# A different hand-out of the work made ahead in a gated layer: value sets, transposes, and weight decoding

## The chip, the cores and the metric

The kernel runs on one core of a Trainium2 chip. The metric is the time of one execution in microseconds (us), as the device measures it. The core's engines work side by side, each through its own queue and in program order: TensorE (PE in the profile, with PEld for its weight loads), VectorE (DVE), ScalarE (ACT), GpSimd (POOL), and SyncE (SP), which here issues most DMAs. They wait for one another through semaphores.

## The reference

The kernel computes three stages one after the other, on 4 x 576 = 2304 tokens of width 512.

```python
scores = scale * q @ k.T;  scores = where(causal, -1e9, scores + decay)      # 4 batches, 8 heads, 576 x 64
x      = softmax(scores) @ v                                                 # -> 2304 x 512
e      = argmax(x @ w_gate + modality_bias[modality_id])                     # one of 8 experts for a token
x      = prob[e] * (relu(x @ w1[e]) @ w2[e])                                 # 512 -> 1024 -> 512
gate   = 1 / (1 + exp(-(x @ moe2_w_gate)))                                   # 512 -> 1536
val    = x @ moe2_w_val                                                      # 512 -> 1536
out    = (gate * val) @ moe2_w_out                                           # 1536 -> 512
```

The three matrices of the last stage are float64 in the input and reach the kernel as pairs of 32-bit words.

## The kernel before

All large products are made in a split form: a float32 matrix is taken apart into a high part (rounded by ScalarE) and a low part (the remainder, by VectorE), and high x high, high x low and low x high are added up in PSUM. So each weight or activation that TensorE reads costs one ScalarE and one VectorE operation first.

**Decoding.** The float64 weights of the gated layer are 36 pieces of 128 x 512 values. `Gated.decode` (L1149) takes a piece through load (SP), one ScalarE operation (L1174), two VectorE operations in its first half (L1155, L1156) and two in its second (L1165, L1166), and a write back to DRAM as float32 (L1161). It is called in halves, and it works as a pipeline: the second half of a call also loads a later piece. The first `AHEAD` pieces are decoded while the experts run: the function `extra` (L1552) is called after each of the eight steps f of an expert unit and gives out as many halves as the table `pace` says for that step. The rest is given out in the gated layer.

**The gated layer** (`Gated.run`, L1429) goes over three strips s of 768 tokens. In a strip there are 12 sets: for each of six column pieces i a gate set (m = 0) and a value set (m = 1). Sets are numbered g = 0 to 35 over all strips, and q = 0 to 11 within a strip. Even sets are gate sets. Sets 0 to 3 make eight products of 6 matmuls directly (`eight`). From set 4 on, `seven` forms the four outputs of a set from seven products of 6 matmuls, called P0 to P6 here, on sums and differences of blocks. The products use two PSUM banks in turn, and what was in a bank must have been read out before the next product goes into it:

- P0 is copied out by ScalarE (L1358) before P2 is added onto it. P2 and P3 are copied out too.
- after P1, P4 and P5, VectorE adds a copied product to the one in PSUM (L1367, L1377, L1380). The add after P4 must have read the bank before P6 is added onto it. The add after P5 must have read its bank before the first product of the next set.
- the last output is read straight out of the bank, by ScalarE's sigmoid (L1337) in a gate set and by VectorE's multiplication with the gate (L1344) in a value set. A value set also splits its four results (L1345, L1346).

**Between the products** the generator yields, and the loop in `run` gives out other work in small portions: `bulk`, a queue of VectorE and ScalarE work made ahead (the next set's weights from `prepare`: L1202, L1205 and the four sums L1214 to L1223; the output weights: L1241, L1244; decode halves; block sums and splits of the next strip: L1292, L1304, L1308), and `outs`, the output products or downs (L1409, 3 matmuls each, 12 after each value set). A portion of `bulk` is its length divided by the steps left in the set (`left`).

**Transposes.** The next strip's 768 rows are loaded (`rows`, L1253), and transposed by `turn` (L1275): three TensorE transposes into one of the two product banks (L1279), a ScalarE copy out of it (L1284). There are eight turns for a strip. In what follows T is a turn and d a down.

Within an engine the order of the program is the order of execution, so work of `bulk` that stands ahead of an add delays this add, and the product that waits for its bank.

Of the kernel before, what the change touches and what calls it, by code (L numbers as in the profile page):

```python
# [29 lines left out]
KD = DM // P  # L30
# [1073 lines left out]
class Gated:  # L1104
# [8 lines left out]
    NB, NH = 768, 384  # L1113
    NP, NS = FF2 // 256, NT // 768

    DIRECT, AHEAD = 4, 24

    STEPS = (0, 0), (1, 1), (4, 2), (3, 3), (5, 4), (6, 5), (2, 6)

# [307 lines left out]
    def run(self, ctx):  # L1427
        self.lp = ctx.enter_context(self.tc.tile_pool(name="ga_l", bufs=1, reuse_waits="tile"))
        self.pp = ctx.enter_context(self.tc.tile_pool(name="ga_p", bufs=1, space=PSUM, reuse_waits="tile"))  # L1429
        self.po = ctx.enter_context(self.tc.tile_pool(name="ga_o", bufs=1, space=PSUM, reuse_waits="tile"))  # L1430
        self.todo.extend(self.late)
        self.flip, self.sg, self.act, self.acts, self.o = 0, {}, {}, {}, {}
        self.defer, outs, bulk = deque(), deque(), deque()
        nset, spare, rests = 2 * self.NP, deque([0, 1] * (len(self.late) + 4)), []
        self.outer_load(0)
        for g, (s, i, m) in enumerate(self.sets):
            q, p = g % nset, self.NP * s + i
            more = s + 1 < self.NS
            if 1 < g + 2 < len(self.sets):
                self.fetch(g + 2)  # L1440
            if m == 1 and p + 1 < self.NP * self.NS:
                self.outer_load(p + 1)
            bulk.extend(self.prepare(g + 1) if g + 1 < len(self.sets) else [])
            if m == 0:
                bulk.extend(self.outer(p))
            if s == 0:
                for _ in range(min(3 if m else 5, len(spare))):
                    bulk.append(lambda h=spare.popleft(): self.decode((h,)))
            if g == 0:
                bulk.extend(self.sums(0))  # L1450
            if g == 2:
                bulk.extend(self.split(0, 2) + self.split(0, 1)[2:] + self.split(0, 3) + self.split(0, 4))
            if more and q == 1:
                self.rows(s + 1)
            if more and q == 4:
                bulk.append(lambda s=s: self.tokens(s + 1))
            if more and q == 8:
                bulk.extend(self.sums(s + 1) + self.split(s + 1, 0))
            if more and q == 10:
                bulk.extend(self.split(s + 1, 1) + self.split(s + 1, 2) + self.split(s + 1, 3))  # L1460
            left = 8 if g < self.DIRECT else 7
            for k, w in enumerate((self.eight if g < self.DIRECT else self.seven)(g)):
                for f in rests:
                    f()
                rests = list(self.defer)
                self.defer.clear()

                x = []
                if g == self.DIRECT - 1 and k == 2:
                    x = self.split(0, 6)  # L1470
                if more and q == nset - 1 and k == 4:
                    x = self.split(s + 1, 4)
                if s and q == 0 and k < 2:
                    x = self.split(s, 5 + k)
                for f in x:
                    f()
                for _ in range(-(-len(bulk) * w // left)):
                    bulk.popleft()()
                left -= w
                for _ in range(w):  # L1480
                    if outs and (len(outs) > 7 - k or not (m == 0 and k in (2, 5) and w == 1)):
                        outs.popleft()()
            if m == 1:
                self.acts[p], self.act = self.act, {}
                order = ((0, 0), (1, 1), (0, 1), (1, 0)) if i + 1 < self.NP else ((1, 1), (0, 1), (0, 0), (1, 0))
                todo = [(r, n, j) for r, n in order for j in range(3)]
                if g + 1 == len(self.sets):
                    todo = [(r, n, j) for n in (1, 0) for j in range(3) for r in ((1, 0) if n else (0, 1))]
                outs.extend(lambda s=s, p=p, z=z: self.down(s, p, *z) for z in todo)
            if more and 3 <= q < 7:  # L1490
                for k in range(2):
                    n, c = divmod(2 * (q - 3) + k, KD)
                    self.turn(s + 1, n, c, self.bank(self.flip ^ k))
                    if outs:
                        outs.popleft()()
        for f in rests:
            f()
        while outs:
            outs.popleft()()
# [9 lines left out]
def decayed_attention_top1_moe_gated_kernel(  # L1509
# [33 lines left out]
    ga = Gated(tc, ro, bits, dram, ps, yd, moe2_w_gate, moe2_w_val, moe2_w_out, out)  # L1543
    none = lambda u, f: None
    with c2:

        pace, todo = (1, 1, 1, 1, 0, 1, 1, 1), deque((0, 1) * (len(ga.todo) + 3))
        turns, first = deque((n, c) for n in range(2) for c in range(KD)), deque()

        def extra(u, f):  # L1550
            if u < NA:
                for _ in range(min(pace[f], len(todo))):  # L1552
                    ga.decode((todo.popleft(),))

            if u == NA - 2 and f == 4:
                ga.rows(0)
            if u == NA - 1 and f == 4:
                ga.tokens(0)
            if u == NA - 1 and f >= 4 or u == NA and f % 2 == 0:
                ga.early(*turns.popleft())  # L1560
            if u == NA and f == 1:
                ga.fetch(0)
            if u == NA and f == 4:
                first.extend(ga.prepare(0))
            if u == NA and f == 5:
                ga.fetch(1)
            if u == NA and f >= 5:
                for _ in range(min(2, len(first))):
                    first.popleft()()

        ex.run(range(1, NA + 1), NA + 1, extra)
        nb = nc.values_load(ro.tl[0:1, 2 * NU:2 * NU + 1], min_val=0, max_val=NB)
        with tc.If(nb > 1):
            ex.run([NA + 1], NA + 1, none)
        with ExitStack() as ifs:
            for u in range(NA + 2, NU):
                ifs.enter_context(tc.If(nb > u - NA))
                ex.start(u)
                ex.run([u], u, none)
# [36 lines left out]
```

## Time and profile before

| | |
|---|---|
| three timed runs | 968.99 us median, 968.35 to 970.5 |
| profiled execution | 972.27 us, span of its instructions 970.6 us |
| TensorE | 920.4 us busy, 95% of the span |
| VectorE | 752.0 us busy, 77% |
| ScalarE | 607.0 us busy, 63% |
| mean granted TensorE clock | 0.98 |

In the profile, a row of the timeline has a start, a length, engine, line, operation and tiles, how many instructions are merged in it, and in brackets the idle time before the row and what ended it. The rows of one engine may overlap a little, because an instruction's pipeline is still draining when the next one starts. The granted clock is 1.00 where TensorE runs at 2.4 GHz and 0.50 where it runs at 1.2 GHz. Attention fills the span up to about 290 us, the experts up to about 509 us, and the gated layer the rest.

### The profile page before, as it was taken

What the parts mean: (1) busy time and instruction counts of PE and PEld (TensorE: products, weight loads), DVE (VectorE), ACT (ScalarE), POOL (GpSimd) and SP (SyncE); (2) the same over time, 40 slices, a digit from 0 to 9 for tenths busy, and PEclk for the clock granted to TensorE, in tenths of its full rate; (3) what the DMA queues carried; (4) which work ended last, traced back from release to release, by engine and by line L of the source; (5) the groups of instructions that cost most, each with busy time, mean ns of one, the idle gap of its engine ahead of it and who ended that gap; (6) DMA issues with size and microseconds to landing.
All of it is one profiled execution on the core that took longest, in us unless ns stands there. A gap on an engine that the chain in (4) does not pass through costs nothing. (4 is left out here: it accounts for less than half of the span.)

```text
span 970.6 us, 17468 instructions
## 1 busy us (share of the span) xinstructions
PE 920.4 (95%) x5679; PEld 844.4 (87%) x5679; DVE 752.0 (77%) x1916; ACT 607.0 (63%) x1355; POOL 291.4 (30%) x560
## 2 busy tenths in 40 slices
PE   4999999899999999999989998899999999999996
PEld 4999998788989999999979887798888898999995
DVE  7888888888796989898876877887665787666662
ACT  5888888678555666666775444565544565555542
POOL 5999998888603222221000000000100000200002
PEclk8999999999999999999999998999999999999998
DMA  6545646536484495558838353322522221421201
GB/s 143 132 132 130 132 105 114 122 86 134 149 205 131 135 350 173 165 162 236 294 119 281 118 190 110 128 66 66 174 66 66 69 76 41 142 66 66 67 21 66
DMA packets 105860, 126.77 MB, mean 131 GB/s; under 512 B 48608, under 2 KB 79840, under 8 KB 105760
## 3 DMA queue, kind: packets, MB, share of 16 engines
q1 hardware_dynamic: 101120, 110.87, 39.4%
q0 software_dynamic: 4640, 14.70, 4.6%
q8 instruction: 46, 0.75, 0.3%
q14 instruction: 54, 0.44, 0.1%
HBM read 127.03 MB, written 24.21 MB: 156 GB/s over the span
## 5 line engine op out<-in xcount | busy, mean ns | idle before, releaser
L1321 PE MATMUL g<-x,wc 128*128 128x384 f32 x1536 | 307.2, 341 | 9.7 <-DVE s L1380 4.2
L1321 PEld LDWEIGHTS g<-x,wc 128*128 128x128 f32 x1536 | 275.1, 189 | 35.6 <-DVE s L1344 6.2
L1409 PE MATMUL o<-wo,ah 128*128 128x512 f32 x648 | 186.7, 400 | 0.2 <-DVE ah L1346 0.2
L1417 POOL DMA_INDIRECT out_dram<-os,tok x18 | 18.6, 1031 | 437.8 <-ACT os L1416 300.5
L1409 PEld LDWEIGHTS o<-wo,ah 128*128 128x128 f32 x648 | 119.7, 190 | 11.8 <-DVE ah L1346 1.0
L1345 ACT ACTIVATE ah<-s 128x384 fp32r<-128x384 f32 x72 | 37.8, 526 | 106.0 <-DVE s L1344 106.0
L257 ACT ACTIVATE sc<-sc,mn 128x576 f32<-128x576 f32 (+4 forms) x160 | 89.3, 561 | 12.6 <-DVE mn L249 12.0
L923 DVE TENSOR_TENSOR wl<-ws,wh 128x1024 fp32r<-128x1024 f32 x80 | 97.1, 1218 | 0.0
L917 ACT ACTIVATE wh<-ws 128x1024 fp32r<-128x1024 f32 x80 | 84.7, 1059 | 18.6 <-PE y L999 18.6
L183 POOL TENSOR_SCALAR dec<-cum 128x576 f32<-128x576 f32 (+4 forms) x160 | 83.6, 532 | 3.9 <-DMA cum<-drow 3.9
L969 POOL DMA_INDIRECT rows_by_expert<-ys,dst x20 | 24.0, 1199 | 196.7 <-ACT ys L968 96.4
L989 PE MATMUL h<-xl,wh 128*128 128x256 f32 x256 | 73.2, 286 | 2.4 <-DVE xl L944 2.4
L279 DVE TENSOR_TENSOR pl<-t,ph 128x512 fp32r<-128x512 f32 x96 | 65.1, 680 | 12.4 <-ACT ph L278 11.6
L989 PE MATMUL h<-xh,wh 128*128 128x256 f32 x256 | 74.3, 290 | 0.0
L989 PE MATMUL h<-xh,wl 128*128 128x256 f32 x256 | 73.1, 285 | 0.0
L1358 ACT ACTIVATE pc<-g 128x384 f32<-128x384 f32 x96 | 46.9, 488 | 40.9 <-PE g L1321 40.5
L249 DVE CUSTOM_DVE_ANT_0 sc<-s,dec 128x192 f32<-128x192 f32 (+4 forms) x160 | 63.9, 409 | 3.7 <-POOL dec L187 2.2
L239 PE MATMUL s<-kh,q 128*128 128x256 f32 (+2 forms) x192 | 59.3, 323 | 4.5 <-DVE mn L249 4.1
L278 ACT ACTIVATE ph<-t 128x512 fp32r<-128x512 f32 x96 | 54.2, 594 | 11.4 <-PE t L268 10.8
L1337 ACT ACTIVATE sg<-sg 128x384 f32<-128x384 f32 x48 | 25.3, 526 | 52.9 <-DVE sg L1380 19.4
L239 PE MATMUL s<-kl,q 128*128 128x256 f32 (+2 forms) x192 | 53.2, 308 | 0.0
L336 PE MATMUL o<-ph,vv 128*128 128x512 f32 (+4 forms) x160 | 52.6, 340 | 0.5 <-ACT ot L349 0.5
(314 smaller groups left out, 2259.4 us busy)
## 6 DMA issues: line engine op xcount, KB each, us to landing
ws<-in_moe_w_dram SPq DMA_DIRECT2D x80, 512.0 KB
wf<-wd SPq DMA_DIRECT2D x36, 512.0 KB
cum<-drow SPq DMA_DIRECT2D x32, 288.0 KB
wd<-dec SPq DMA_DIRECT2D x18, 512.0 KB
wof<-wd SPq DMA_DIRECT2D x18, 512.0 KB
raw<-in_moe_w_gate_dram SPq DMA_DIRECT2D x12, 512.0 KB
raw<-in_moe_w_val_dram SPq DMA_DIRECT2D x12, 512.0 KB
raw<-in_moe_w_out_dram SPq DMA_DIRECT2D x12, 512.0 KB
```

What stands on the lines that cost most here:

```text
L183: nc.gpsimd.tensor_scalar(t[0:m, DO[b]:DO[b] + W[b]], c[0:m, 0:W[b]], -1.0, c[0:m, R0[b]:R0[b] + 1], ALU.mult, ALU.add)
L239: nc.tensor.matmul(ps[0:M[b], o:o + w], q2[:, j, R0[b]:R0[b] + M[b]], kk[:, j, c0:c0 + w], start=(i == 0), stop=(i == 1),)
L249: nc.vector.tensor_tensor_reduce(s[0:m, SO[b] + c0:SO[b] + c1], t[b, c0][:, 0:c1 - c0], d[0:m, DO[b] + c0:DO[b] + c1], -1.0, mn[0:m, 5:6] ...
L257: nc.scalar.activation(so, so, AF.Exp, bias=mn[0:m, b:b + 1], scale=-1.0, accum_out=sm[0:m, c:c + 1])
L278: nc.scalar.activation(ph[0:m, o:o + w], t, AF.Copy)
L279: nc.vector.tensor_tensor(pl[0:m, o:o + w], t, ph[0:m, o:o + w].bitcast(F32), ALU.subtract)
L336: nc.tensor.matmul(dst, v[:, c], p[i][:, a:b], start=start and i == 0, stop=stop and i == 1)
L917: self.nc.scalar.activation(hi, self.wraw(u, k), AF.Copy)
L923: ins = eng.tensor_tensor(lo, self.wraw(u, k), hi.bitcast(F32), ALU.subtract)
L989: nc.tensor.matmul(t, a[:, c, cs], b[:, c, :], start=(n == 0), stop=(n == 3 * KD - 1))
L1321: self.nc.tensor.matmul(t, p[:, c, :], q[:, c, :], start=(first and n == 0), stop=(n == total - 1), skip_group_check=not first)
L1409: nc.tensor.matmul(o[0], x[:, cs], y[:, r, :], start=(o[1] == 0 and k == 0), stop=(o[1] == 2 * self.NP - 1 and k == 2))
```

## The change

Five things are changed, all in the code that gives out work.

- `AHEAD` goes from 24 to 28 pieces, and `pace` gives a decode half to step f = 4 of an expert unit too. So 28 instead of 24 pieces are decoded during the experts, and in sets 0 to 7 each gate set takes 4 halves (5 before), each value set 2 (3 before).
- in value sets from set 4 on, `left` starts at 4 instead of 7: `bulk` is given out behind P0 to P3, and nothing of it behind P4 to P6.
- the eight turns of a strip were made two at a time behind the sets q = 3, 4, 5, 6. Now four are made behind q = 4 and four behind q = 6, both gate sets.
- `rows` of the next strip is called at q = 0 instead of q = 1.
- splits and sums are interleaved, so that the ScalarE part of one stands ahead of the VectorE part of another.

```diff
-    DIRECT, AHEAD = 4, 24
+    DIRECT, AHEAD = 4, 28
...
-                for _ in range(min(3 if m else 5, len(spare))):
+                for _ in range(min(2 if m else 4, len(spare))):
...
-                bulk.extend(self.split(0, 2) + self.split(0, 1)[2:] + self.split(0, 3) + self.split(0, 4))
-            if more and q == 1:
+                a, b, c, d = self.split(0, 2), self.split(0, 1)[2:], self.split(0, 3), self.split(0, 4)
+                bulk.extend(a[:1] + c[:1] + b + a[1:] + d[:1] + c[1:] + d[1:])
+            if more and q == 0:
                 self.rows(s + 1)
...
-                bulk.extend(self.sums(s + 1) + self.split(s + 1, 0))
+                a = self.split(s + 1, 0)
+                bulk.extend(a[:1] + self.sums(s + 1) + a[1:])
...
-                bulk.extend(self.split(s + 1, 1) + self.split(s + 1, 2) + self.split(s + 1, 3))
-            left = 8 if g < self.DIRECT else 7
+                a, b, c = (self.split(s + 1, k) for k in (1, 2, 3))
+                bulk.extend(a[:1] + b[:1] + a[1:2] + c[:1] + b[1:] + a[2:] + c[1:])
+
+            left = 8 if g < self.DIRECT else 4 if m else 7
...
-                for _ in range(-(-len(bulk) * w // left)):
+                for _ in range(-(-len(bulk) * w // left) if bulk else 0):
...
-            if more and 3 <= q < 7:
-                for k in range(2):
-                    n, c = divmod(2 * (q - 3) + k, KD)
-                    self.turn(s + 1, n, c, self.bank(self.flip ^ k))
+            if more and q in (4, 6):
+                for a in range(KD * (q // 2 - 2), KD * (q // 2 - 1)):
+                    self.turn(s + 1, *divmod(a, KD), self.bank(self.flip))
+                    self.flip ^= 1
...
-        pace, todo = (1, 1, 1, 1, 0, 1, 1, 1), deque((0, 1) * (len(ga.todo) + 3))
+        pace, todo = (1, 1, 1, 1, 1, 1, 1, 1), deque((0, 1) * (len(ga.todo) + 3))
```

The first place is TensorE's order from the turns behind gate set 4 to the end of value set 5. L1321 with x6 is one product, L1279 a turn, L1409 a down. Before:

```order
L1279 MATMUL g<-ident,y 128x128 x3
L1409 MATMUL o<-wo,ah 128x512 x3
L1279 MATMUL g<-ident,y 128x128 x3
L1409 MATMUL o<-wo,ah 128x512 x3
L1321 MATMUL g<-x,wc 128x384 x6
L1409 MATMUL o<-wo,ah 128x512 x3
L1321 MATMUL g<-x,wc 128x384 x36
L1279 MATMUL g<-ident,y 128x128 x3
L1409 MATMUL o<-wo,ah 128x512 x3
L1279 MATMUL g<-ident,y 128x128 x3
L1409 MATMUL o<-wo,ah 128x512 x3
```

The same place of the changed kernel, up to the first product of set 6:

```order
L1279 MATMUL g<-ident,y 128x128 x3
L1409 MATMUL o<-wo,ah 128x512 x3
L1279 MATMUL g<-ident,y 128x128 x3
L1409 MATMUL o<-wo,ah 128x512 x3
L1279 MATMUL g<-ident,y 128x128 x3
L1409 MATMUL o<-wo,ah 128x512 x3
L1279 MATMUL g<-ident,y 128x128 x3
L1409 MATMUL o<-wo,ah 128x512 x3
L1321 MATMUL g<-x,wc 128x384 x6
L1409 MATMUL o<-wo,ah 128x512 x3
L1321 MATMUL g<-x,wc 128x384 x42
```

The two turns behind value set 5 have gone to the gate set ahead of it, and P1 to P6 of set 5 are followed at once by the first product of set 6; one down is left within set 5, as before.

The second place is VectorE's order in value set 5, in its later part: L1205 are low parts of the next set's weights, L1155 to L1166 decoding, L1377 the add after P4, L1380 the add after P5, L1344 a multiplication with the gate. Before:

```order
L1220 TENSOR_TENSOR ws<-wf 128x256
L1205 TENSOR_TENSOR wc<-wf,wc 128x256
L1377 TENSOR_TENSOR s<-pc,g 128x384
L1344 TENSOR_TENSOR s<-sg,s 128x384
L1205 TENSOR_TENSOR wc<-ws,wc 128x512 x2
L1380 TENSOR_TENSOR s<-pc,g 128x384
L1344 TENSOR_TENSOR s<-sg,s 128x384
L1346 TENSOR_TENSOR ah<-s,ah 128x384
L1165 SCALAR_TENSOR_TENSOR dec<-raw,dec 128x512
L1166 SCALAR_TENSOR_TENSOR dec<-raw,dec 128x512
L1344 TENSOR_TENSOR s<-sg,g 128x384
```

The same place of the changed kernel:

```order
L1220 TENSOR_TENSOR ws<-wf 128x256
L1205 TENSOR_TENSOR wc<-wf,wc 128x256
L1205 TENSOR_TENSOR wc<-ws,wc 128x512 x2
L1155 TENSOR_SCALAR dec<-dec 128x512
L1156 TENSOR_SCALAR dec<-dec 128x512
L1165 SCALAR_TENSOR_TENSOR dec<-raw,dec 128x512
L1166 SCALAR_TENSOR_TENSOR dec<-raw,dec 128x512
L1377 TENSOR_TENSOR s<-pc,g 128x384
L1344 TENSOR_TENSOR s<-sg,s 128x384
L1380 TENSOR_TENSOR s<-pc,g 128x384
L1344 TENSOR_TENSOR s<-sg,s 128x384
```

Two weight parts and a whole piece of decoding now stand ahead of the add after P4, and nothing but the set's own results stands behind it.

## Rows read from the trace of the kernel before

**Rows 1.** Busy time of the engines, granted clock and DMA in stretches of the span.
```profile
290.00:505.00 215.00, 214.13 (x1386) 193.63 (x1386) 183.95 (x322) 145.39 (x231) 43.39 (x35) 0.99 0.63 199
...
552.00:564.00 12.00, 9.65 (x35) 8.17 (x34) 9.01 (x20) 4.39 (x10) 0.00 (x0) 0.72 0.53 175
...
584.00:596.00 12.00, 9.42 (x37) 8.23 (x38) 7.84 (x17) 4.78 (x10) 0.00 (x0) 0.72 0.55 175
596.00:620.00 24.00, 21.47 (x112) 18.88 (x111) 19.91 (x41) 12.29 (x26) 0.00 (x0) 1.00 0.22 79
```

**Rows 2.** Waits of TensorE in the gated layer: us in total, times, longest.
```profile
PE g L1279 <- DVE s L1344: 5.5, 4, 2.4
PE g L1321 <- DVE s L1380: 4.2, 3, 1.5
```

**Rows 3.** The chain that ended last: one product and one down.
```profile
644.26 1.05 PE g L1321 x6
...
650.53 0.70 PE o L1409 x3
```

**Rows 4.** Timeline from the end of set 3 to set 4.
```profile
551.06 1.03 DVE L1308 TENSOR_TENSOR x<-b,x 128x384 fp32r<-128x384 f32 x2 [0.54 <-ACT x L1304]
...
552.34 1.28 DVE L1205 TENSOR_TENSOR wc<-ws,wc 128x512 fp32r<-128x512 f32 x2
553.54 0.55 DVE L1344 TENSOR_TENSOR s<-sg,g 128x384 f32<-128x384 f32 x1
...
554.15 0.55 PE L1279 MATMUL g<-ident,y 128*128 128x128 f32 x3 [1.54 <-DVE s L1344]
...
556.20 2.29 PE L1321 MATMUL g<-x,wc 128*128 128x384 f32 x6 [0.81 <-ACT b L1284]
```

**Rows 5.** Timeline of TensorE in value set 5 and the turns behind it.
```profile
575.45 7.18 PE L1321 MATMUL g<-x,wc 128*128 128x384 f32 x36
584.18 0.55 PE L1279 MATMUL g<-ident,y 128*128 128x128 f32 x3 [1.55 <-DVE s L1380]
...
587.83 0.90 PE L1279 MATMUL g<-ident,y 128*128 128x128 f32 x3 [2.40 <-DVE s L1344]
```

**Rows 6.** Timeline of TensorE in value set 7 and into set 8.
```profile
610.80 3.73 PE L1321 MATMUL g<-x,wc 128*128 128x384 f32 x18 [0.15 <-ACT pc L1358]
616.06 1.32 PE L1321 MATMUL g<-x,wc 128*128 128x384 f32 x6 [1.53 <-DVE s L1380]
...
618.92 1.32 PE L1321 MATMUL g<-x,wc 128*128 128x384 f32 x6 [0.84 <-DVE s L1344]
```

**Rows 7.** VectorE's decoding in the gated layer, by form: mean ns of one.
```profile
L1166 DVE SCALAR_TENSOR_TENSOR dec<-raw,dec 128x512 int32<-128x512 int32 x9 | 6.2, 692 | 0.3
...
L1156 DVE TENSOR_SCALAR dec<-dec 128x512 int32<-128x512 int32 x8 | 3.4, 427 | 0.3
```

**Rows 8.** Timeline of value sets 17 and 19: P1 onwards, and a turn.
```profile
731.54 6.90 PE L1321 MATMUL g<-x,wc 128*128 128x384 f32 x36
...
740.60 0.55 PE L1279 MATMUL g<-ident,y 128*128 128x128 f32 x3 [0.89 <-DVE s L1344]
...
757.72 8.25 PE L1321 MATMUL g<-x,wc 128*128 128x384 f32 x42
```

**Rows 9.** Timeline at the end of value set 11.
```profile
664.27 0.42 DVE L1205 TENSOR_TENSOR wc<-wf,wc 128x256 fp32r<-128x256 f32 x1
664.60 0.55 DVE L1380 TENSOR_TENSOR s<-pc,g 128x384 f32<-128x384 f32 x1
...
665.19 0.56 DVE L1344 TENSOR_TENSOR s<-sg,s 128x384 f32<-128x384 f32 x1
665.21 1.34 PE L1321 MATMUL g<-x,wc 128*128 128x384 f32 x6 [1.33 <-DVE s L1380]
```

**Rows 10.** Timeline of VectorE at step f = 5 of an expert unit.
```profile
447.69 0.69 DVE L944 TENSOR_TENSOR xl<-x,xh 128x512 fp32r<-128x512 f32 x1 [0.49 <-ACT xh L943]
```

**Rows 11.** Timeline of ScalarE in set 0, at the output weights.
```profile
515.72 1.15 ACT L1241 ACTIVATE wo<-wof 128x512 fp32r<-128x512 f32 x2 [0.84 <-DMA wof<-wd]
```

## The prediction

> **What bounds the kernel now.** I read the stretches first, because a share of busy time over the whole span mixes three stages. In the experts TensorE is busy 214.13 of 215 us and VectorE 183.95 [rows 1]: nothing there is lost, and VectorE has about 31 us to spare. In the gated layer the reader should look for two things, idle TensorE and a low clock. The list of TensorE's waits names VectorE's read-outs of a product bank as the cause of nearly all idle time: turns that waited for the multiplication L1344 (four waits, 5.5 us) and products that waited for the add after P5, L1380 (three, 4.2 us) [rows 2]. The timeline puts them in value sets, or behind them. In two stretches, 552 to 564 and 584 to 596 us, the clock is 0.72 on average [rows 1], a mix of the levels 1.2 and 2.4 GHz. Each costs 0.28 x 12 = 3.4 us on top of the waits. Otherwise the gated layer is bound by TensorE: a product is 1.05 us and a down 0.70 [rows 3], and neither their number nor that of the turns changes. So the sum is over waits.
>
> VectorE is late in sets 3 to 8 since it has more to do there than TensorE. In a value set it makes three adds, four multiplications, four low parts of about 0.55 and 4.2 us of weights, 10.3 us in all, and decoding comes on top. A whole piece of decoding is 2 x 0.43 + 2 x 0.69 = 2.2 us [rows 7]. Yet sets 5 and 7 have 7 products and one down, 8.1 us.
>
> **The change part by part.**
>
> *Decoding moved to the experts.* Four pieces, 4 x 2.2 = 8.9 us of VectorE, go to 8 expert units, 1.1 us in each. VectorE's spare 31 us are waits for ScalarE, and the new half stands at one of them: just ahead of the low part that waited 0.49 us at f = 5 [rows 10]. Its first operations (0.85 us) fill that wait. What is left, some 0.4 us, is absorbed by further waits of the unit. I cost it at 0, and the cover is that TensorE hardly waits in this stage. If nothing were covered it would cost 8.9, if the shifted halves help a little, -0.5. I take 0 since it is nearest to the 215 us row. Four more loads and two more writes of 512 KB go through SP and the DMA engines, which are 0.63 busy there [rows 1]. SP waits in order behind each, but expert weights are loaded several steps ahead. Cost 0, or 1 us at worst.
>
> *Rows loaded at q = 0.* Six loads stand ahead of two decode loads and of the weights of set 3 in SP's queue. The one DMA that ScalarE waited for there is `wof`, 0.84 us [rows 11], which is issued ahead of them. The cover is that sets 0 and 1 have no downs and little VectorE work. Cost 0, between -0.8 (that wait gone) and +1.7 (as long again and half a bank wait).
>
> *Sets 3 and 4.* Before, the second turn behind set 3 waited 1.54 us for the multiplication at 553.54, the first product of set 4 another 0.81, and the clock fell: 1.54 + 0.81 + 3.4 = 5.7 us [rows 1, 4]. Now set 4's P0 follows at once, at 551.4. The multiplication is a little earlier, because the portion ahead of it is 0.34 + 0.34 + 0.60 instead of 0.33 + 1.20 (two 512-wide parts in 1.28 us start 0.60 apart [rows 4], a 256-wide one 0.33 [rows 9]): it ends at 553.85. P1 needs that bank and could start at 551.4 + 1.05 + 0.70 = 553.15: 0.7 us of wait. Behind it VectorE has two low parts (0.95), a weight part (0.60), a piece of decoding (2.25) and a sum (0.34) before the add after P1, which ends at 553.3 + 0.5 + 4.1 + 0.55 = 558.45. P3 needs that bank and could start at 557.4: 1.05 us. Together 1.8. **Gain 3.9.**
>
> *Set 5.* Before: 36 matmuls took 7.18 us instead of 6.3 + 0.1, so 0.8, then 1.55 and 2.40 at the turns [rows 5], and 3.4 of clock: 8.1. Now the turns are gone from here, and the four of them behind set 4, with their downs, give VectorE time to catch up. But the whole portion stands ahead of the add after P4. I count VectorE from the end of P1. In the rows a dependent 384-wide operation starts 0.59 after the one before [rows 9], an independent one about 0.47. So: start 0.28, add 0.59, multiplication 0.48, sum 0.34, 512-wide part 0.60, sum 0.34, low part 0.47, sum 0.34, 256-wide part 0.34, two 512-wide 1.20: 4.98. Decoding 2.25, add 0.55 and its signal 0.05: 7.8. TensorE has P2 to P5 in this time, 4.2 us, and then P6 must wait 3.6 us. Behind P6 nothing is late: the add after P5 ends at about 8.9, and P6 at 8.9. **Gain 8.1 - 3.6 = 4.5**, if the clock holds.
>
> *Set 7.* Before 0.15 + (3.73 - 3.25) + 1.53 + 0.84 = 3.0 us [rows 6]. Now no decoding is left for it, as the last call finds its pipeline empty, and the same count gives 4.98 + 0.60 = 5.6 against 4.2. **Gain 3.0 - 1.4 = 1.6.**
>
> *Sets 11 and 23.* The first product of set 12 waited 1.33 us for the add L1380, which stood behind a split and a 256-wide part of 0.33 us [rows 9]. This part is now made earlier, the split stays. The third of the waits for L1380 [rows 2] is the same at set 24. **Gain 2 x 0.33 = 0.7.** In sets 9, 13 and the other value sets a down stands behind each of P0 to P4, TensorE needs 4.2 + 4 x 0.7 = 7.0 us from P1 to P6, and 5.6 suffices: 0, before and now.
>
> *Sets 15, 17, 19.* The turn behind 15 waited 5.5 - 1.54 - 2.40 - 0.89 = 0.7 us [rows 2, 4, 5, 8]. **Gain 0.7.** Set 17 lost 6.90 - 6.4 = 0.5 and 0.89 at its turn [rows 8], 1.4, and now loses 1.4 as set 7 does: 0. Set 19 lost 8.25 - 7.45 = 0.8 (P1 to P6 and one product of set 20 [rows 8]) and will lose 1.4: **loss 0.6.**
>
> *Four turns behind a gate set.* The first needs the add after P5 and the second ScalarE's sigmoid, both over while P6 and a down run; the third needs the copy of the first, over one turn and one down later. 0, or 0.3 each for 16 turns at worst, 5 us. The interleaved splits change only which engine is asked first: 0, or 0.5 either way.
>
> Sum: 3.9 + 4.5 + 1.6 + 0.7 + 0.7 - 0.6 = 10.8 us. The profiled execution took 972.27, with 1.7 us around its span of 970.6, so it would take 961.5. The timed median, 968.99, is 3.3 us below it. If that difference stays, the median becomes 958.2. It is also about the price of one fall of the clock (3.4). If the timed runs had one fall less, they lose that part of the gain, and 961.5 is the time. I take 959.0, near the first.
>
> **Where the clock decides.** Two waits of 1.54 and 0.81 us were followed by a fall [rows 1, 4]. Two of 1.53 and 0.84 in set 8 were not, the clock is 1.00 from 596 to 620 [rows 1, 6]. So waits of this size are on the edge. The changed kernel has one larger (3.6 at set 5), two close together at set 4, and three of 1.4. The Trainium skill (page "TensorE: Matmul & The Clock Gate", section "A second HAM failure mode: psum-queue depth-cycling") says that short idle times between groups of matmuls that cycle through PSUM banks can make the clock go back and forth. By that rule the value sets 5, 7, 17 and 19 would each bring a fall, 13.4 us in all. The trace bears it out at sets 3 and 5 and not at 7, 17 and 19, so it is a rival below and no term of the sum.
>
> **Rivals.**
> 1. *One fall stays, at set 5.* For: its 3.6 us are longer than any wait of the gated layer before. Against: it is one wait with full work on both sides. Time 959.0 + 3.4 = 962.4.
> 2. *The experts take it back.* The new half at f = 4 makes the hidden activation's low part late at f = 7, in eight units. For: VectorE is 0.86 busy there. Against: 31 us of spare time for 8.9. If all of it shows, 959.0 + 8.9 = 967.9.
> 3. *Slower: the clock falls in every value set without downs.* Place: P6 of sets 5, 7, 17, 19. Price 3.4 each, 13.4 in all, so 959.0 + 13.4 = 972.4. It decides from the third on: three give 969.2 (no change), four are slower. Against: waits of 1.3 to 1.5 us alone had no fall before.
> 4. *The change does not do what it says* is excluded: the orders show turns and decoding moved.
>
> **How the numbers follow.** Forecast (no fall, 955 to 961.5) 0.56. Rival 1, up to 965: 0.26. Rival 2 in part or whole: 0.10, half of it within 0.2% (1.9 us, what a measurement of this kernel can tell from no change). Rival 3: 0.08, of which 0.06 slower and 0.02 the same. Faster 0.56 + 0.26 + 0.05 = 0.87, same 0.07, slower 0.06. Range 955 to 966.5: below, the waits that I worked out (1.8 + 3.6 + 3 x 1.4 = 9.6) are a third smaller; above, rival 1 with some of the turns' bound.
>
> **What would show it.** Right: no low clock at 552 to 564; no wait of a turn for L1344; in set 5 a wait of P6 for L1377 of 3 to 4 us; 1.2 to 1.6 at P6 of sets 7, 17 and 19; 1.0 at sets 12 and 24; the experts' stretch as long as now. Wrong: TensorE waiting for L960 or L923 in the experts, a stretch at 1.2 GHz behind set 5, or turns that wait for ScalarE.

## The result and the profile after

The changed kernel takes 958.83 us (median of 4 runs, 957.4 to 960.99), the kernel before 969.45 in the runs beside it (4 runs). The ratio is 0.989, 95% interval 0.987 to 0.992: 10.6 us faster. The profiled execution took 959.55 us, with a span of 957.8.

Busy time and granted clock in four stretches of the changed kernel, the experts first. The columns are those of [rows 1].

```profile
290.00:505.00 215.00, 214.10 (x1385) 193.50 (x1385) 190.89 (x336) 147.68 (x235) 45.43 (x35) 1.00 0.66 213
550.00:562.00 12.00, 10.65 (x54) 9.29 (x54) 11.83 (x25) 7.71 (x16) 0.00 (x0) 1.00 0.25 87
576.00:588.00 12.00, 10.11 (x38) 9.31 (x39) 8.82 (x19) 3.97 (x9) 0.00 (x0) 0.72 0.22 87
588.00:612.00 24.00, 22.99 (x124) 20.75 (x123) 17.91 (x37) 13.29 (x27) 0.00 (x0) 1.00 0.25 88
```

VectorE does 6.9 us more in the experts (183.95 before, [rows 1]) and TensorE's busy time is the same. The low clock at 552 is gone. At the end of set 5 there still is one.

TensorE's waits in the gated layer, against [rows 2]: us in total, times, longest.

```profile
PE g L1321 <- ACT pc L1358: 2.9, 6, 0.6
PE g L1321 <- DVE s L1377: 2.8, 3, 1.9
...
PE g L1321 <- DVE s L1380: 1.8, 2, 0.9
PE g L1321 <- DVE sg L1367: 0.8, 1, 0.8
PE g L1321 <- DVE s L1344: 0.6, 1, 0.6
```

No turn waits any more. New is a wait for L1358, ScalarE's copies of P2 and P3, which the prediction had not named.

The timeline of TensorE from set 3 to set 4, against [rows 4]:

```profile
551.40 0.86 PE L1409 MATMUL o<-wo,ah 128*128 128x512 f32 x3
552.82 1.34 PE L1321 MATMUL g<-x,wc 128*128 128x384 f32 x6 [0.55 <-DVE s L1344]
554.00 0.86 PE L1409 MATMUL o<-wo,ah 128*128 128x512 f32 x3
554.70 1.22 PE L1321 MATMUL g<-x,wc 128*128 128x384 f32 x6
555.75 0.86 PE L1409 MATMUL o<-wo,ah 128*128 128x512 f32 x3
557.41 1.31 PE L1321 MATMUL g<-x,wc 128*128 128x384 f32 x6 [0.80 <-DVE sg L1367]
```

And of set 5 from P1 into set 6, against [rows 5]:

```profile
570.33 3.33 PE L1321 MATMUL g<-x,wc 128*128 128x384 f32 x18
574.11 1.33 PE L1321 MATMUL g<-x,wc 128*128 128x384 f32 x6 [0.44 <-ACT pc L1358]
575.98 1.32 PE L1321 MATMUL g<-x,wc 128*128 128x384 f32 x6 [0.55 <-ACT pc L1358]
579.20 4.21 PE L1321 MATMUL g<-x,wc 128*128 128x384 f32 x12 [1.89 <-DVE s L1377]
```

A number in brackets is less than what is lost. A product's row lasts 1.22 to 1.34 us where products follow each other every 1.05, and a bracket counts only from the later end of the row before it. By the starts, P1 to P6 take 579.20 - 570.33 = 8.87 us instead of 5 x 1.05 = 5.25: 3.6 us are lost, while the brackets add up to 2.88. Of the 3.6 us, P6 loses 2.2 (579.20 - 575.98 - 1.05), and P4 and P5 lose 1.4 behind ScalarE's copies. The last row is P6 and the first product of set 6: 12 matmuls in 4.21 us, at 1.2 GHz.

VectorE in the same set: the add after P1, the piece of decoding (first and last row), the add after P4.

```profile
571.66 0.56 DVE L1367 TENSOR_TENSOR s<-pc,g 128x384 f32<-128x384 f32 x1 [3.79 <-PE g L1321]
...
576.35 0.42 DVE L1155 TENSOR_SCALAR dec<-dec 128x512 f32<-128x512 f32 x1
...
577.99 0.69 DVE L1166 SCALAR_TENSOR_TENSOR dec<-raw,dec 128x512 int32<-128x512 int32 x1
578.60 0.55 DVE L1377 TENSOR_TENSOR s<-pc,g 128x384 f32<-128x384 f32 x1
```

VectorE has no gap between 571.66 and 579.15, and the piece of decoding is 2.25 us of it.

The columns below are lengths from the first product of one set to the first of a later one (the starts of the L1321 rows), two sets together so that a turn moved from one to the next cancels.

| sets | before | after | gain | worked out |
|---|---|---|---|---|
| 3, 4 | 33.53 | 29.47 | 4.1 | 3.9 |
| 5, 6 | 31.90 | 30.85 | 1.05 | 4.5 |
| 7, 8 | 23.89 | 21.86 | 2.0 | 1.6 |
| 11, 12 and 23, 24 | 50.21 | 48.63 | 1.6 | 0.7 |
| 15, 16 | 28.17 | 27.24 | 0.9 | 0.7 |
| 17, 18 | 26.19 | 25.88 | 0.3 | 0 |
| 19, 20 | 21.40 | 21.80 | -0.4 | -0.6 |
| 9, 10, 13, 14, 21, 22 | 70.43 | 69.44 | 1.0 | 0 |
| 25 to 35 | 127.76 | 126.35 | 1.4 | 0 |
| all 36 | 444.33 | 432.42 | 11.9 | 10.8 |

Set 35 is counted up to the start of its last matmul. Of the rest of the profiled difference of 12.7 us, 1.1 lies ahead of the gated layer (its first product starts at 508.21 instead of 509.29), and 0.2 goes back behind its last one.

### The profile page after: what moved, and what is told of

It reads as the page before. It is cut to its first block, busy times and chain, and to the rows that moved or that the text cites. A ratio compares the mean times of both kernels' runs of the same rounds, so it can differ in the third digit from the quotient of the medians.

```text
span 957.8 us, 17435 instructions
## 1 busy us (share of the span) xinstructions
PE 913.7 (95%) x5679; PEld 842.6 (88%) x5679; DVE 752.8 (79%) x1916; ACT 607.0 (63%) x1355; POOL 294.5 (31%) x560
## 5 line engine op out<-in xcount | busy, mean ns | idle before, releaser
L1321 PE MATMUL g<-x,wc 128*128 128x384 f32 x1536 | 305.0, 340 | 11.4 <-ACT pc L1358 2.9
L1321 PEld LDWEIGHTS g<-x,wc 128*128 128x128 f32 x1536 | 275.3, 189 | 33.2 <-ACT pc L1358 4.8
L1409 PE MATMUL o<-wo,ah 128*128 128x512 f32 x648 | 185.1, 398 | 0.2 <-DVE ah L1346 0.2
L1409 PEld LDWEIGHTS o<-wo,ah 128*128 128x128 f32 x648 | 118.4, 188 | 11.7 <-DVE ah L1346 1.0
L1345 ACT ACTIVATE ah<-s 128x384 fp32r<-128x384 f32 x72 | 37.9, 526 | 101.7 <-DVE s L1344 98.8
L1358 ACT ACTIVATE pc<-g 128x384 f32<-128x384 f32 x96 | 46.5, 484 | 33.0 <-PE g L1321 32.9
L278 ACT ACTIVATE ph<-t 128x512 fp32r<-128x512 f32 x96 | 54.1, 593 | 10.8 <-PE t L268 10.4
L989 PEld LDWEIGHTS h<-xl,wh 128*128 128x128 f32 x256 | 49.6, 194 | 4.0 <-DVE xl L944 2.6
```

Of the source, the lines that this page charges most:

```text
L278: nc.scalar.activation(ph[0:m, o:o + w], t, AF.Copy)
L989: nc.tensor.matmul(t, a[:, c, cs], b[:, c, :], start=(n == 0), stop=(n == 3 * KD - 1))
L1321: self.nc.tensor.matmul(t, p[:, c, :], q[:, c, :], start=(first and n == 0), stop=(n == total - 1), skip_group_check=not first)
L1358: nc.scalar.activation(c, t, AF.Copy)
L1409: nc.tensor.matmul(o[0], x[:, cs], y[:, r, :], start=(o[1] == 0 and k == 0), stop=(o[1] == 2 * self.NP - 1 and k == 2))
```

## The experiments

Lengths as in the table above. In five kernels of this section (turns, value sets, no decoding in set 5, and the last two) set 0 takes 10.0 us instead of 8.5, at a low clock. No edit touches that place, and the groups below begin behind it.

| kernel | ratio to before, 95% | sets 3 to 8 | 9 to 14 | 15 to 20 | 21 to 35 |
|---|---|---|---|---|---|
| before | 1 | 89.32 | 72.15 | 75.75 | 176.25 |
| changed | 0.989, 0.987 to 0.992 | 82.18 | 70.61 | 74.92 | 173.81 |
| turns alone | 0.995, 0.993 to 0.997 | 83.54 | 72.17 | 74.38 | 176.24 |
| value sets alone | 0.994, 0.992 to 0.995 | 85.52 | 70.61 | 75.69 | 173.81 |
| decoding alone | 0.994, 0.992 to 0.996 | 83.69 | 72.15 | 75.75 | 176.24 |
| rows and splits alone | 1.000, 0.999 to 1.002 | 87.05 | 72.17 | 75.75 | 176.32 |
| changed, value sets undone | 0.990, 0.989 to 0.992 | 79.82 | 72.17 | 74.37 | 176.32 |

**One part at a time, on the kernel before.** Turns:

```diff
-            if more and 3 <= q < 7:
-                for k in range(2):
...
+            if more and q in (4, 6):
+                for a in range(KD * (q // 2 - 2), KD * (q // 2 - 1)):
...
```

> The kernel before with the turns alone moved behind the gate sets q = 4 and 6. Theory A (each part of the change removes the bank waits that it names): the waits of turns behind sets 3, 5, 15 and 17 go, and with them the fall of the clock behind set 3; products of set 4 still wait some 3 us for banks, as three halves of decoding stand at the end of set 3, and set 5 keeps a wait of about 1.5 us for the add after P5 and perhaps its fall. Gain 8 us with one fall left (about 961.5), 11 without. Theory B (the gain comes from four pieces of decoding less beside the gated layer): the turns' waits move to the next products, gain under 2 us (967.5 or more).

Measured 965.19 us, between the two theories. The waits of the turns went, and in this profile no fall is left behind set 3 or set 5. But in place of the two turns behind set 5, which waited 1.55 and 2.40 us [rows 5], the first two products of set 6 now wait, 1.54 us for L1380 and 1.63 for L1344, and a product of set 4 waits 1.24 for L1367: theory B is right about where a part of the time goes.

Value sets:

```diff
-            left = 8 if g < self.DIRECT else 7
+            left = 8 if g < self.DIRECT else 4 if m else 7
```

> The kernel before with the hand-out of value sets in four steps alone. Theory A: the two waits of L1380 at sets 12 and 24 shrink by 0.4 us each, the 0.2 to 0.4 us that every gate set behind a value set lost go (about 3 us), the turns behind sets 15 and 17 no longer wait (1.2), but sets 5 and 7 get waits of P6 of 5 and 2.5 us, and both falls of the clock stay. Gain 4 to 6 us, about 964.5. Theory B: no gain beyond 2 us, or a loss, since as much work as before stands ahead of the adds.

Measured 963.81 us, as theory A has it, a little above its 4 to 6 us. By the starts P1 to P6 lose 4.6 us in set 5 and 2.35 in set 7, where 5 and 2.5 were expected.

Decoding:

```diff
-    DIRECT, AHEAD = 4, 24
+    DIRECT, AHEAD = 4, 28
...
-                for _ in range(min(3 if m else 5, len(spare))):
+                for _ in range(min(2 if m else 4, len(spare))):
...
-        pace, todo = (1, 1, 1, 1, 0, 1, 1, 1), ...
+        pace, todo = (1, 1, 1, 1, 1, 1, 1, 1), ...
```

> The kernel before with 28 pieces decoded during the experts alone. Theory A: the experts do not get longer; sets 5 and 7 lose 1.3 and 1.2 us less, set 3 nearly as much as before; gain 2.5 to 3 us if both falls of the clock stay (about 966.5), 3.4 more for each that goes. Theory B: this is most of the gain, 8 us or more (961 or less).

Measured 964.7 us; between 290 and 505 us TensorE is busy for 214.09 of 215 us, as before [rows 1], so four pieces more in the experts cost nothing. The gain of 5.5 us lies between the theories. The fall behind set 3 went, but one came in set 8 that the kernel before does not have. The first product of set 8 waits 1.53 us in both and has a row of 1.32 us before [rows 6], but 2.11 here, where the clock is 0.86 from 608 to 620 us:

```profile
609.15 2.11 PE L1321 MATMUL g<-x,wc 128*128 128x384 f32 x6 [1.53 <-DVE s L1380]
608.00:620.00 12.00, 10.85 (x48) 10.03 (x49) 8.64 (x18) 6.26 (x13) 0.00 (x0) 0.86 0.16 61
```

Alone the three parts bring 5.0, 6.4 and 5.5 us, 16.9 together, where the change brings 10.6. The table says where the overlap is: in sets 3 to 8 they save 5.8, 3.8 and 5.6 us each alone, 15.2, but 7.1 together, since each removes some of the same waits and falls. In sets 9 to 14 and 21 to 35 nothing overlaps: only the value sets' part gains there, and its 1.5 and 2.4 us appear in the changed kernel to the last digit. In sets 15 to 20 the turns alone save 1.4 us, but the changed kernel only 0.8, as sets 17 and 19 have the value sets' new waits there.

With the value sets' part alone, P4 and P5 (first row) and P6 of set 5:

```profile
576.41 2.37 PE L1321 MATMUL g<-x,wc 128*128 128x384 f32 x12 [0.97 <-ACT pc L1358]
581.98 2.29 PE L1321 MATMUL g<-x,wc 128*128 128x384 f32 x6 [3.19 <-DVE s L1377]
```

So this part by itself makes the new wait for L1377, and a fall follows here too (x6 in 2.29 us).

**Rows and splits alone.**

```diff
-            if more and q == 1:
+            if more and q == 0:
                 self.rows(s + 1)
...
-                bulk.extend(self.sums(s + 1) + self.split(s + 1, 0))
+                a = self.split(s + 1, 0)
+                bulk.extend(a[:1] + self.sums(s + 1) + a[1:])
...
```

> The kernel before with the two small parts of the change alone: the next strip's rows loaded one set earlier, and splits and sums interleaved. Theory A (they only change which engine is asked first, nothing waits for them): every set within 0.1 us of before but sets 1 to 4, 11 and 23, together within 1 us, 970. Theory B (the earlier loads hold up the decode loads and the weights in the queue): sets 1 to 3 longer by up to 1.7 us, 972. Theory C (the interleaved splits take away the 0.3 us at sets 11 and 23 and some of the wait at set 3): 968.5.

Measured 969.16 us against 969.33. Sets 1 and 2 and from 7 on are as before within 0.1 us. Sets 4 and 6 are 1.5 and 0.8 us shorter. In set 4 this is a shorter fall of the clock (0.86 on average, against 0.72 in [rows 1]):

```profile
550.00:562.00 12.00, 9.63 (x44) 8.24 (x43) 9.92 (x22) 5.88 (x13) 0.00 (x0) 0.86 0.51 169
```

At set 5 the fall begins earlier, and the second turn waits 1.67 us instead of 2.40. The timed runs do not show these 2.3 us, so they belong to the two profiled executions and not to the edit. Neither the 1.7 us of theory B nor the gain of theory C at sets 11 and 23 (12.38 in both kernels) came. This leaves theory A.

**The value sets' part taken back in the changed kernel.**

```diff
-            left = 8 if g < self.DIRECT else 4 if m else 7
+            left = 8 if g < self.DIRECT else 7
```

> The changed kernel with one part taken back: in value sets the work made ahead is again given out over seven products instead of four. Theory A (each part is worth what its own waits are worth, and parts share sets): the later gate sets take 12.44 us again instead of 12.22 (ten of them, +2.2), sets 12 and 24 0.4 more each, sets 11, 13, 23 and 25 0.3 to 0.4 more each (together +4.6), but sets 17 and 19 return to 8.68 from 9.53 and the wait of P6 in set 5 goes, with the fall of the clock behind it (12.71 to about 10.3): -4.1, and set 7 +0.4. So about 959.7, no more than 1 us over the changed kernel's 958.8. Theory B (this part brings on top of the others what it brings alone, 6.4 us): 965.

Measured 959.58 us, as theory A has it: on top of the other parts it brings nothing that can be measured. It gives 1.6 and 2.5 us in the later sets (the gate sets go back to 12.44), and costs 2.4 in sets 3 to 8 and 0.55 in sets 15 to 20, where its waits, and at set 5 the fall, go with it.

**Decode halves of sets 0 to 7 as 6 and 0 instead of 4 and 2.**

```diff
-                for _ in range(min(2 if m else 4, len(spare))):
+                for _ in range(min(0 if m else 6, len(spare))):
```

> The changed kernel with six decode halves in each gate set of the first strip and none in value sets (4 and 2 in the changed kernel). Theory A: the wait of P6 of set 5 (1.9 us, behind a piece of decoding) goes, the fall of the clock behind it goes too (3.4), and set 4 loses the 0.8 us at P3: 6 us faster than the changed kernel, about 953; gate sets 4 and 6 hide the added 2.2 us of VectorE under their 16 us. Theory C (the fall of the clock has another cause than this wait): only 2.7 us faster, about 956, with 6.8 us at 1.2 GHz still behind set 5. Theory D (VectorE is then late in the gate sets): no gain or a loss.

Measured 959.0 us: no gain. The wait at P6 of set 5 and the fall behind it went, and set 5 took 10.1 us. But set 4 rose from 18.2 to 21.3, and sets 1 and 2 by 2.3 together. ScalarE and TensorE behind set 4:

```profile
570.58 0.66 ACT L1174 ACTIVATE dec<-raw 128x512 f32<-128x512 f32 x1 [3.42 <-DMA raw<-in_moe_w_out_dram]
```

```profile
571.68 0.55 PE L1279 MATMUL g<-ident,y 128*128 128x128 f32 x3 [3.23 <-ACT b L1284]
```

The third decoding of a set reads a load that the first one issued, and it is not there yet. ScalarE waits with the copies of the turns queued behind, and TensorE waits for a copy. Theory A is right about set 5, theory D about the time.

**No decoding in set 5, without three decodings in one set.**

```diff
-                for _ in range(min(2 if m else 4, len(spare))):
+                for _ in range(len(spare) and min((4, 2, 4, 2, 5, 0, 5, 2)[g] if g < 8 else 0, len(spare))):
```

> The changed kernel, but the decode halves of sets 0 to 7 are 4, 2, 4, 2, 5, 0, 5, 2 instead of 4, 2, 4, 2, 4, 2, 4, 2: none in set 5. Theory A (VectorE's piece of decoding ahead of the add after P4 makes the wait of 1.89 us at P6 of set 5, and the fall of the clock follows this wait): set 5 takes about 10.1 us instead of 12.71, no fall behind it, sets 4 and 6 as now since only two decodings in each read a load: about 956.3. Theory B (moving decoding only moves its wait for the loads, as with 6 and 0 halves, where set 4 took 3.1 us longer): set 4 or 6 loses 1 to 3 us, 958 to 960.

Measured 956.01 us, ratio 0.986 (0.984 to 0.988). TensorE in set 5, and the stretch around it:

```profile
572.66 3.33 PE L1321 MATMUL g<-x,wc 128*128 128x384 f32 x18
576.44 2.37 PE L1321 MATMUL g<-x,wc 128*128 128x384 f32 x12 [0.44 <-ACT pc L1358]
579.28 2.37 PE L1321 MATMUL g<-x,wc 128*128 128x384 f32 x12 [0.47 <-DVE s L1377]
```

```profile
574.00:586.00 12.00, 11.09 (x59) 9.99 (x58) 11.56 (x25) 6.76 (x15) 0.00 (x0) 1.00 0.29 107
```

P1 to P6 lose 579.28 - 572.66 - 5.25 = 1.4 us instead of 3.6, and the clock stays at 2.4 GHz: the 12 matmuls of the last row take 2.37 us instead of 4.21. Sets 3 to 8 take 77.76 instead of 82.18, 4.4 us less: sets 5 and 6 4.8 less, of which 2.2 are the wait and the other 2.5 the fall, and sets 3 and 4 0.4 more. This is theory A. The medians differ by 2.8 us only; in the profile of this kernel, 1.5 of the 4.4 us are lost again in set 0, at the low clock named above.

**Work given out over five products instead of four.**

```diff
-            left = 8 if g < self.DIRECT else 4 if m else 7
+            left = 8 if g < self.DIRECT else 5 if m else 7
```

> The changed kernel with the work made ahead given out behind five products of a value set instead of four, so that the last low part stands behind the add after P4 and not ahead of it. Theory A (P6 waits only for what stands on VectorE ahead of that add): the waits at P6 of sets 7, 17 and 19 (0.57, 0.46, 0.46) go and that of set 5 falls from 1.89 to about 1.3, the later gate sets stay at 12.22 because nothing stands behind the add after P5: -2.1, about 956.7. Theory B (the part then delays the add after P5 and the last multiplications, so that the first two products of the next set wait as long): the value sets get shorter by 0.5, the gate sets behind them longer by as much, 958.8.

Measured 973.61 us, ratio 1.005 (1.003 to 1.007): 15 us slower than the changed kernel, against both theories. The first line of TensorE's waits is now

```profile
PE g L1321 <- DVE s L1380: 16.3, 14, 2.2
```

VectorE and ScalarE behind P4 of set 27, and the first product of set 28:

```profile
854.32 0.56 DVE L1344 TENSOR_TENSOR s<-sg,s 128x384 f32<-128x384 f32 x1
854.79 0.69 DVE L1205 TENSOR_TENSOR wc<-ws,wc 128x512 fp32r<-128x512 f32 x1
854.91 0.53 ACT L1345 ACTIVATE ah<-s 128x384 fp32r<-128x384 f32 x1 [1.95 <-DVE s L1344]
855.34 0.61 ACT L1202 ACTIVATE wc<-ws 128x512 fp32r<-128x512 f32 x1
855.99 0.69 DVE L1205 TENSOR_TENSOR wc<-ws,wc 128x512 fp32r<-128x512 f32 x1 [0.51 <-ACT wc L1202]
856.60 0.55 DVE L1380 TENSOR_TENSOR s<-pc,g 128x384 f32<-128x384 f32 x1
857.20 1.32 PE L1321 MATMUL g<-x,wc 128*128 128x384 f32 x6 [0.76 <-DVE s L1380]
```

I had thought that the last low part (0.6 us) would move behind the add after P4. Two low parts and a high part of ScalarE moved. The high part stands on ScalarE behind L1345, which waits for the multiplication; the last low part waits for the high part; the add after P5 waits behind the low part. This chain goes twice between the two engines, and it delays the next set in every value set, also in those with downs, where before nothing waited: sets 9, 27 and the like take 11.8 us instead of 10.9, sets 17 and 19 10.8 and 10.5 instead of 9.5.

In set 5 of this kernel P6 no longer waits long, but the first product of set 6 does:

```profile
580.69 1.31 PE L1321 MATMUL g<-x,wc 128*128 128x384 f32 x6 [1.99 <-DVE s L1380]
```

This wait is longer than that of P6 in the changed kernel (1.89 us), one product later, and yet no fall follows: the clock is 1.00 from 576 to 588 us.

**The last low part behind P6, no decoding in set 5.**

```diff
-            bulk.extend(self.prepare(g + 1) if g + 1 < len(self.sets) else [])
+            parts = self.prepare(g + 1) if g + 1 < len(self.sets) else []
+            last = [parts.pop()] if parts and m and g >= self.DIRECT else []
+            bulk.extend(parts)
...
-                for f in x:
+                for f in x + (last if k == 6 else []):
```

> The changed kernel with no decoding in set 5 (4, 2, 4, 2, 5, 0, 5, 2 halves in sets 0 to 7), and with the last low part of the next set's weights given out behind P6 of a value set instead of behind P3. Theory A (P6 waits for what stands on VectorE ahead of the add after P4): the waits of 0.46 to 0.57 at P6 of sets 5, 7, 17 and 19 go, and nothing else moves, since this low part is first read at P4 or P5 of the next set: the four sets take 9.1 instead of 9.53, 1.9 us less than without the edit, about 954.1. Theory B (as with five products: a ScalarE high part in front of it still holds up the add after P5, or the part delays the read-outs of the next gate set): no gain, 956 or above.

Measured 954.5 us, ratio 0.984 (0.981 to 0.987). P4 to the first product of set 18:

```profile
720.58 4.61 PE L1321 MATMUL g<-x,wc 128*128 128x384 f32 x24 [0.45 <-ACT pc L1358]
```

The wait at P6 is gone. Sets 17 and 19 take 8.9 us instead of 9.5, set 5 9.1 instead of 9.5. Set 7 did not change: what waits there is P5, for ScalarE, and not P6, as I had written. This is theory A in three of the four sets. The interval overlaps that of the kernel without the edit (0.984 to 0.988), so the gain is seen in the profile alone: 0.4 us in set 5 and 0.6 each in sets 17 and 19.

**In addition the first result's high part behind the copy of P2.**

```diff
-        nc.scalar.activation(a[:, 0], o, AF.Copy)
-        self.defer.append(lambda: V(a[:, 1], o, a[:, 0].bitcast(F32), ALU.subtract))
+        hi = lambda: nc.scalar.activation(a[:, 0], o, AF.Copy)
+        lo = lambda: V(a[:, 1], o, a[:, 0].bitcast(F32), ALU.subtract)
+        if make is not None and (r, n) == (0, 0) and direct is None:
+            self.defer.append(lambda: (hi(), self.defer.append(lo)))
+        else:
+            hi()
+            self.defer.append(lo)
```

> The kernel with the last low part behind P6 and no decoding in set 5, and in addition the high part of a value set's first result is made behind the copy of P2 on ScalarE, not ahead of it, its low part one product later. Theory A (the waits of 0.44 to 0.46 at P4 and part of those at P5 are this copy standing behind a high part that waits for VectorE): P4 and P5 of sets 5, 7, 17 and 19 no longer wait, these sets take 8.6 us instead of 9.1, 952.3. Theory B (the time comes back at P6, because the add after P4 stands at the end of the same VectorE work whatever P4 does): same as the kernel without this edit, 954.

Measured 953.28 us, ratio 0.982 (0.980 to 0.984), the lowest median here, 5.6 us below that of the changed kernel (0.8% by the ratios, as the kernel before took 971.29 us in these runs). Its interval lies wholly below that of the changed kernel. P1 to P5 and P6 of set 17 (L1382 is the add after P4 in this kernel's own lines):

```profile
716.76 5.56 PE L1321 MATMUL g<-x,wc 128*128 128x384 f32 x30
722.76 2.37 PE L1321 MATMUL g<-x,wc 128*128 128x384 f32 x12 [0.45 <-DVE s L1382]
```

The wait at P4 has gone to P6 with its size, and set 17 takes 8.92 us as without the edit: theory B there and in set 19. Set 7 gains 0.5, set 5 0.15. Between this kernel and the one above the intervals overlap, so the gain of this last edit, too, is seen in the profile alone.

## Why the prediction was right, and where its steps were not

The time was right, 959.0 against 958.83, but partly by luck, because two errors nearly cancel: sets 5 and 6 gained 3.4 us less than the sum has, and 4.6 us of small gains came that it did not contain. The stretch at 1.2 GHz behind set 5, which the prediction names as a sign of being wrong, came in the profile. Its price for that case, 962.4, was too high.

*Sets 3 and 4: right.* The low clock is gone. By the starts, set 4 loses 552.82 - 551.40 - 0.70 = 0.7 us at P1 and 557.41 - 554.70 - 1.05 - 0.70 = 1.0 at P3, for the 0.7 and 1.05 worked out. The gain is 4.1, not 3.9. But it depends on the execution: against the profile with rows and splits alone, where the fall behind set 3 is half as long, sets 3 and 4 gain 2.5 (32.02 to 29.47).

*Set 5: the wait right, the clock wrong.* The wait was worked out as 3.6 us and is 3.6 in all, and VectorE's work up to the add after P4 sets it, as the prediction says. The sign that it names, 3 to 4 us at P6 for L1377, did not come: 1.89 stand there, and the rest is spent earlier, behind ScalarE's copies. The condition "if the clock holds" failed: rival 1, to which I had given 0.26, is what happened in the profiled execution, and this is the step that failed. In the kernel without decoding in set 5, P1 to P6 lose 1.4 us and no fall comes, and with the value sets undone set 5 takes 10.5, without a fall. So the fall goes when this wait goes, in each kernel here that shortens it; with the value sets' part alone the wait is longer still, and a fall follows. Why the clock fell behind this wait, and not behind the 1.99 us of the kernel with five products, stays open. Each kernel has one profile, so how often the fall comes in the timed runs of the changed kernel is not known either.

*What the fall before had cost there* was also too high by about 0.8. I took 0.28 x 12 us from the stretch's clock. But the stretch contains idle time, where a low clock costs nothing: TensorE stands still up to 587.83 at the turn [rows 5]. That idle time as a stretch of its own, in the kernel before:

```profile
585.43:587.83 2.40, 0.01 (x1) 0.01 (x1) 2.33 (x6) 0.43 (x2) 0.00 (x0) 0.68 0.25 14
```

The clock was low for most of it and cost nothing. The loss of 8.1 us was 7.25: 31.90 less the 24.65 that sets 5 and 6 would take without the waits of set 5. The 24.65 is an estimate, the 26.07 of the kernel with no decoding in set 5 less the 1.42 that its set 5 takes above its 8.1 us of products and downs. Of the 3.4 us missing at sets 5 and 6, this is 0.8 and the new fall 2.5.

*Sets 7, 17 and 19: the size right, the place in part.* 1.4 us was worked out for each, at P6. By the starts, P1 to P6 lose 1.6 in set 7 and 1.4 in sets 17 and 19. P1 to P6 of set 17 in the changed kernel, against [rows 8]:

```profile
720.89 3.33 PE L1321 MATMUL g<-x,wc 128*128 128x384 f32 x18
724.66 2.38 PE L1321 MATMUL g<-x,wc 128*128 128x384 f32 x12 [0.45 <-ACT pc L1358]
727.50 2.37 PE L1321 MATMUL g<-x,wc 128*128 128x384 f32 x12 [0.46 <-DVE s L1377]
```

727.50 - 720.89 - 5.25 = 1.4. That half of it would appear at P4, behind ScalarE's copy, the prediction did not say; in sets 17 and 19 the last experiment shows that it makes no difference, because VectorE's work up to the add sets when P6 can start. In set 7 nearly all of it stands at P4 and P5 behind these copies, and there the last experiment gains 0.5. No fall followed in the three. So rival 3 had the right sort of event, a fall behind the wait of a value set without downs, but it came in one set of the four, the one with 3.6 us. The Trainium skill (page "TensorE: Matmul & The Clock Gate", section "A second HAM failure mode: psum-queue depth-cycling") says that short idle times between groups of matmuls on cycling PSUM banks can make the clock go back and forth; the traces here agree for set 5 and not for sets 7, 17 and 19, where 1.4 to 1.6 us were lost at 2.4 GHz.

*The missing term: the gate sets behind value sets.* I cost the other value sets at 0, and the gate sets had no term at all, as the list of waits has no row for them. TensorE and VectorE of the kernel before, from the end of set 25:

```profile
837.80 0.69 DVE L1205 TENSOR_TENSOR wc<-ws,wc 128x512 fp32r<-128x512 f32 x1
...
838.17 0.86 PE L1409 MATMUL o<-wo,ah 128*128 128x512 f32 x3
838.41 0.55 DVE L1344 TENSOR_TENSOR s<-sg,g 128x384 f32<-128x384 f32 x1
...
839.01 1.32 PE L1321 MATMUL g<-x,wc 128*128 128x384 f32 x6
```

and the same place of the changed kernel:

```profile
825.91 0.55 DVE L1344 TENSOR_TENSOR s<-sg,g 128x384 f32<-128x384 f32 x1
826.28 0.86 PE L1409 MATMUL o<-wo,ah 128*128 128x512 f32 x3
...
826.98 1.22 PE L1321 MATMUL g<-x,wc 128*128 128x384 f32 x6
```

Before, a low part stood ahead of the last multiplication, P1 started 0.84 us after the down instead of 0.70, and the next row came 0.1 later behind it: some 0.22 us. No bracket stands there, because the row of the down before it ends only at 839.03, after the product has started. Gate sets from 26 on went from 12.44 to 12.22, and eight gate sets in all gain 0.22 to 0.24. Sets 11 to 13 and 23 to 25, also with less behind P4 to P6, gain 0.3 to 0.4 each where 0.33 was worked out for each pair. The value sets' part alone gives these lengths, and undoing it takes them back. With the few tenths more in sets 3, 7 and 15 to 20 these make the 4.6 us.

*Decoding in the experts at 0, rows and splits at 0, four turns at 0: right.* The decoding alone leaves the experts as long as they were, rows and splits alone change nothing in the timed runs, and no turn waits. Rival 2 did not happen.

*The median.* I held the profile's 961.5 and the median's 958.2 apart, and took 959.0. The profile gave 959.55 and the median 958.83, so most of the 3.3 us between the two before went away. The profiled execution before had one low clock more in attention, at about 221 us, which the changed kernel's does not have. The profile with rows and splits alone (968.54 us, its median 969.16) bears on this: it has 1.5 us less than the profile before ahead of the gated layer and 2.3 less in sets 4 and 6. So the profile that I worked from had more and longer falls than this one. Subtracting gains counted in it from a median 3.3 us lower came out by luck as much as by reason.

## What to carry to other kernels

A loss of 0.2 us in each of many places stands in no list of waits: compare the starts of equal steps with the sum of their products, set by set, before saying that a stretch loses nothing. When parts of a change help at the same waits, their gains alone do not add (16.9 us here, 10.6 together), and one of them can be worth nothing on top of the others. A profile is one execution: two of nearly the same kernel differed by 2.3 us through the clock alone, so a gain from a fall that goes should be held against the timed runs. Work made ahead must be placed by what the next engine's queue holds, too: a part that was to go behind an add brought a ScalarE operation with it and made the kernel 15 us slower, while the single low part with no reader before the next set's P4 could go to the end, at a gain of 0.4 to 0.6 us in three sets of the profile.

## What the runs showed of the hardware

- A wait's bracket is smaller than the loss: 2.88 us of brackets for 3.6 lost in set 5, 0.91 for 1.4 in set 17. 
- How long TensorE waited does not alone tell whether the clock falls: 3.6 us in set 5 had a fall, as did 3.2 at a turn of the kernel with 6 and 0 halves, and 1.4 to 1.6 us did not in sets 7, 17 and 19; before, 1.54 and 0.81 had one and 1.53 and 0.84 had none [rows 1, 4, 6]. A single wait of 1.53 at set 8 had one with decoding alone, and 1.99 at set 6 had none with five products.
- The fall at set 5 of the changed kernel cost about 2.5 us rather than 3.4, in part because 0.7 us of the 6.8 at 1.2 GHz lay in the wait.
- The clock fell in set 0 in five of the ten experiments' profiles and not in the others, without a difference in the work there: 1.5 us that no edit explains. TensorE's idle time just ahead of set 0 was 2.9 to 3.1 us in these five; in the others it was 2.6 to 2.7, but 2.97 with decoding alone, which had no fall there.
